# Pairs of tokens side by side in a result, and one store of 128 partitions for each result

## The chip, the cores and the metric

The kernel runs on one core of a Trainium2 chip. The metric is the device time of one execution in microseconds. Before the change the median of three runs is 188.31 us, and the runs lie between 187.92 and 189.54 us. The profile shows one further execution, which took 188.43 us.

## The reference, cut to what matters

```
kv  = einsum('bhsd,bhse->bhde', k, v)          # 8 batches, 8 heads, 576 tokens, 64 per head
o   = einsum('bhsd,bhde->bhse', q, kv)
a   = o / sqrt(mean(o*o, -1) + 1e-6) * g_norm  # per token and head
x   = a with the heads of a token side by side # 4608 tokens x 512
h   = x @ w_in                                 # 512 x 1024
u   = h * softmax(h)
ln  = (u - mean(u)) / sqrt(var(u) + 1e-6) * g_ln
out = ln @ w_out                               # 1024 x 512, float32
```

## The kernel before, in words

The 4608 tokens are worked through in nine chunks of 512. Chunk c from 0 to 7 is a batch without the last ninth of its tokens: the 576 tokens of a batch are read as 64 rows p of nine tokens j, and the chunk holds the tokens with j from 0 to 7. The tokens with j = 8 of all eight batches are copied into q_last and make chunk 8. A chunk has two halves of heads (hf) and two halves of tokens (z or g, the parity of j).

The order of all work is written out by hand, as a list of words called ORDER: each engine's instructions stand in the order of this list, so every queue is in order and a piece that waits holds what is behind it on its engine. A second list, HOME, gives each tile of PSUM one of eight banks. A tile waits for the tile that had its bank before.

A chunk passes these steps, with their words in ORDER and their lines:

- *q*, *k*, *v* (L318) are loads that POOL issues, and they cast to bf16. *kv_mm* (L378) makes kv, and *kv* copies it to kvd.
- *qT* turns q. For chunks 0 to 4 it is a TensorE transpose (L416). For chunks 5 to 8 it is a DMA transpose on SP's queue (L425).
- *o_mm* (L443) makes o, transposed: a head's 64 values in partitions, tokens in columns. For chunks 0 to 7 one product writes 256 columns (four j by 64 p), for chunk 8 it writes 64.
- *sq* squares o on ScalarE (L236), *s_mm* (L501) takes means over a head by a product, *ln* (L505) and *ex* (L509) make the reciprocal root on ScalarE, and *x* (L521) multiplies o, g_norm and this root on VectorE and writes x in bf16.
- *h* is the product with w_in. In chunks 0 to 3 (L574) x is the moving operand and d_ff lies in partitions. In chunks 4 to 8 (L603) x is the stationary operand and tokens lie in partitions.
- *exp* or *expt* (L581, L611) on ScalarE and *u* or *ut* (L585, L617) on VectorE make u. *usq* (L238) and *es* (L598) on POOL, *sums* (L685) on TensorE, or *bn* (L623) on VectorE, make the statistics, *stats* and *rstd* the factor of each token.
- *turnu* (L639) turns u by DMA, in two halves, for chunks 4 to 8, on SP's queue.
- *out* (L751) is the product with w_out, in four blocks m of 128 tokens. *ob* scales it by rstd on VectorE (L244) or ScalarE (L242) into a tile of the four buffers ob.
- *store* writes a block to memory. SP issues nearly all of them (L769); three of chunk 8's five are issued from ScalarE's queue (L765).

A block of 128 tokens of chunks 0 to 7 holds two values of j, 64 tokens each, one below the other: partitions 0 to 63 have j = 2(2(m%2)) + m//2, and partitions 64 to 127 have the j that is 2 larger. So a block leaves as two stores of 64 partitions, with rows of 2 KB:

```
for x in range(2):
    j = 2 * (2 * (m % 2) + x) + m // 2
    on[engine].dma_start(
        out[c * S:c * S + S, :].rearrange("(p j) d -> j p d", j=9)[j], t[64 * x:64 * x + 64, :]
    )
```

SP's queue has the stores and the DMA transposes in one order, as ORDER has them.

Of the kernel before, what the change touches and what calls it, by code (L numbers as in the profile page):

```python
# [99 lines left out]
o.5.0.1:7 s.5.0.0:1 s.5.0.1:0 o.5.1.0:1 o.5.1.1:2 s.5.1.0:3 s.5.1.1:0 o.6.0.0:5 o.6.0.1:0 s.6.0.0:1 s.6.0.1:7  # L100
o.6.1.0:7 o.6.1.1:5 s.6.1.0:1 s.6.1.1:0 o.7.0.0:3 o.7.0.1:2 s.7.0.0:6 s.7.0.1:6 o.7.1.0:7 o.7.1.1:5 s.7.1.0:6
s.7.1.1:2 o.8.0.0:4 o.8.0.1:0 s.8.0.0:6 s.8.0.1:1 o.8.1.0:2 o.8.1.1:6 s.8.1.0:3 s.8.1.1:3 h.4.0.0:3 h.4.0.1:3
h.4.1.0:2 h.4.1.1:7 h.4.2.0:1 h.4.2.1:6 h.4.3.0:5 h.4.3.1:6 h.5.0.0:5 h.5.0.1:7 h.5.1.0:0 h.5.1.1:6 h.5.2.0:4
h.5.2.1:5 h.5.3.0:1 h.5.3.1:0 h.6.0.0:2 h.6.0.1:5 h.6.1.0:7 h.6.1.1:0 h.6.2.0:6 h.6.2.1:1 h.6.3.0:3 h.6.3.1:0
h.7.0.0:3 h.7.0.1:1 h.7.1.0:6 h.7.1.1:7 h.7.2.0:0 h.7.2.1:7 h.7.3.0:2 h.7.3.1:0 h.8.0.0:7 h.8.0.1:3 h.8.1.0:3
h.8.1.1:7 h.8.2.0:6 h.8.2.1:1 h.8.3.0:5 h.8.3.1:7 h.0.0:3 h.0.1:4 h.0.2:2 h.0.3:4 h.0.4:0 h.0.5:6 h.0.6:4 h.0.7:5
# [3 lines left out]
out.2.1:5 out.2.2:0 out.2.3:0 out.3.0:3 out.3.1:4 out.3.2:4 out.3.3:2 out.4.0:7 out.4.1:4 out.4.2:0 out.4.3:3  # L110
out.5.0:5 out.5.1:7 out.5.2:2 out.5.3:3 out.6.0:6 out.6.1:0 out.6.2:5 out.6.3:1 out.7.0:5 out.7.1:0 out.7.2:3
out.7.3:1 out.8.0:5 out.8.1:1 out.8.2:7 out.8.3.0:5 out.8.3.1:7 s.warm:3
# [10 lines left out]
TOKA = ()  # L123

# [53 lines left out]
def kernel(  # L178
# [131 lines left out]
    def heads(c):  # L310
        return (slice(0, 4), slice(4, 8)) if c < 2 else (slice(0, 8),)

    def part_of(c, hf):
        return hf if c < 2 else 0
# [48 lines left out]
    def kv_pairs(b, x):  # L363
        return slice(2 * x, 2 * x + 2) if b < 2 else slice(x, NP, 2)
# [4 lines left out]
    def kv_mm(b, xs):  # L369
        for m in range(2):  # L370
            for i in range(9):
                for x in xs:
                    n = range(NP)[kv_pairs(b, x)][m]
                    for r in range(2):
                        rows = slice(64 * r, 64 * r + 64)
                        for w in range(2) if b < 2 else (0,):
                            y = r ^ (w if b < 2 else x)
# [6 lines left out]
    def kv_copy(engine, b, x, part):  # L384
        if b < 2:
            copy(engine, kvd[:, b, part, kv_pairs(b, x), :], T[kv_key(b, x, part)][:, :, :])
            return
# [7 lines left out]
    def kv_parts(b):  # L395
        return range(2 if b < 2 else 3)

    for b in range(B):
        for xs in ((0,), (1,)) if b < 2 else ((0, 1),):
            g = xs[0]  # L400
            key = {(x, part): kv_key(b, x, part if b < 2 else 0) for x in xs for part in kv_parts(b)}
# [32 lines left out]
    def o_mm(c, hf):  # L434
        qT = T["qT", c]
        for pp in range(2):
            n = 2 * hf + pp
            for y in [slice(0, 4)] if c < B else range(4):
                for hh in range(2):
                    for g in range(2):  # L440
                        first = q_block(c, n, g)
                        rows = slice(64 * g, 64 * g + 64)
                        nc.tensor.matmul(  # L443
                            bank(("o", c, hf, g), [128, 2, 4, 64])[hh * 64:hh * 64 + 64, pp, y, :],
# [23 lines left out]
    def ot_sum(c, y2):  # L468
        sq, s = T["rst", ("sq", c, y2)], kept_tile(("es", ("ss", c, y2)), [128, 2, H, D // 2], FP32)
        a, width = sq, D // 2  # L470
        while width:
            nc.gpsimd.tensor_tensor(out=s[:, :, :, 0:width], in0=a[:, :, :, 0:width], in1=a[:, :, :, width:2 * width], op=ADD)
            a, width = s, width // 2

    def ot_rsqrt(c, y2):
        s, rh = T["es", ("ss", c, y2)], kept_tile(("rh", (c, y2)), [128, 2, H], FP32)
        nc.scalar.activation(out=rh[:, :, :], in_=s[:, :, :, 0], func=AF.Ln, scale=1.0 / D, bias=eps_t[:, :])
# [17 lines left out]
    def o_sq(engine, *i):  # L495
        t = kept_tile(("osq", i), [128, 512], BF16)
        square(engine, t[:, :], T[("o", *i)].rearrange("p a b c -> p (a b c)"))
# [9 lines left out]
    def s_exp(*i):  # L507
        t = kept_tile(("rst", i), [128, 2, 4, 64], FP32)
        nc.scalar.activation(  # L509
            out=t.rearrange("p a b c -> p (a b c)"), in_=T["lss", i][:, :], func=AF.Exp, scale=-0.5, bias=zero_t[:, :]  # L510
        )

    def s_rsqrt(*i):
        t = kept_tile(("rst", i), [128, 2, 4, 64], FP32)
        nc.scalar.activation(
            out=t.rearrange("p a b c -> p (a b c)"), in_=T["s", i][:, :], func=AF.Abs_reciprocal_sqrt, bias=eps_t[:, :]
        )

    def x_mul(c, hf, z):
        t = kept_tile(("x", c), [128, NP, 2, 4, 64], BF16)  # L520
        nc.vector.scalar_tensor_tensor(  # L521
            out=t[:, 2 * hf:2 * hf + 2, z], in0=T["o", c, hf, z][:, :, :, :], scalar=g_rep,
            in1=T["rst", (c, hf, z)][:, :, :, :], op0=MUL, op1=MUL,
# [4 lines left out]
    for c in range(NC):  # L528
# [3 lines left out]
        if c in TOKA:  # L532
            for y2 in range(2):
# [7 lines left out]
                add(("rh", c, y2), "act", lambda _, a=(c, y2): ot_rsqrt(*a), [("ssum", c, y2), "table"], [ss, rh])  # L541
# [6 lines left out]
        for hf in range(2):  # L548
# [5 lines left out]
            kvs = [("kv", b, x, part) for b in ([c] if c < B else range(B)) for x in ((hf,) if b < 2 else range(2))  # L554
# [17 lines left out]
    def h_mm(c, f, dts):  # L572
        for dt in dts:
            nc.tensor.matmul(  # L574
                bank(("h", c, f), [128, 512])[:, :], w_in_sb[:, dt, f * 128:(f + 1) * 128],
                T["x", c][:, dt].rearrange("p a b c -> p (a b c)"), start=(dt == 0), stop=(dt == NP - 1),
# [23 lines left out]
    def ht_mm(c, m, g):  # L600
        x = T["x", c]
        for dt in range(NP):
            nc.tensor.matmul(  # L603
                bank(("h", c, m, g), [128, 512])[:, :], x[:, NP * (m ^ 2 * odd(c, dt)) + dt, :] if c in TOKA else
                x[:, dt, m // 2 ^ odd(c, dt), 2 * (m % 2):2 * (m % 2) + 2, :].rearrange("p b c -> p (b c)"),
# [150 lines left out]

    def scale(engine, key, cols):
        c, m = key[1:3]
        t = kept_tile(("ob", c, m), [128, d_model], FP32)
        times(engine, t[:, cols], T[key][:, cols], T["rstd", c][:, m:m + 1])  # L760

    def store(engine, c, m, cols):
        t = T["ob", c, m]
        if c == LAST:
            on[engine].dma_start(out.rearrange("(r j) d -> j r d", j=9)[8, 128 * m:128 * m + 128, cols], t[:, cols])  # L765
            return
        for x in range(2):
            j = 2 * (2 * (m % 2) + x) + m // 2
            on[engine].dma_start(  # L769
                out[c * S:c * S + S, :].rearrange("(p j) d -> j p d", j=9)[j], t[64 * x:64 * x + 64, :]  # L770
            )
# [77 lines left out]
```

## Time and profile before

| | |
|---|---|
| profiled execution, whole | 188.43 us |
| its span, in which the profile has instructions | 186.7 us |
| TensorE matmul busy | 171.0 us (92%) |
| ScalarE busy | 143.7 us (77%) |
| VectorE busy | 134.9 us (72%) |
| POOL busy | 73.2 us (39%) |
| mean granted TensorE clock | 0.997 |
| stores from SP, count and size | 65 issues (64 of L769), 128 KB at the median |
| stores from SP, issue to landing, median | 2.7 us |
| DMA transposes of u, issue to landing, median | 4.4 us |
| L521, the product that makes x | 36 times, 746 ns in the mean |

The span is counted from the first instruction to the last that the profile shows. The rest of the execution, 1.7 us, lies around it. Busy shares are means over the whole span, and the stages differ; the views by window tell them apart. A row of the timeline gives the start, the duration, the engine, the line, the operation with its operands, the count, and in brackets how long the engine was idle before it and what ended that.

### The profile page before, as it was taken

Reading aid. Unit: us, or ns where it says so; the run is one execution under the profiler, and the core shown is the slowest. Engines: PE = TensorE matmul, PEld = TensorE weight load, DVE = VectorE, ACT = ScalarE, POOL = GpSimd, SP = SyncE. Lnnn points to the kernel's source line nnn. Section 1 sums busy time; section 2 is a strip of 40 time slices with the busy share of each in tenths; the row PEclk is TensorE's granted clock in tenths of the full one; section 3 lists DMA queues with packets and bytes.
Section 4 is the critical chain, followed back from the end, with each engine's and each line's share of the span. In section 5 each row is a group of like instructions: output and inputs, shape, how many; then the busy total and the mean of one; then the engine's idle time right before and its main releaser. Section 6 shows DMA issues by size and latency. Waiting matters only on the chain.

```text
span 186.7 us, 4938 instructions
## 1 busy us (share of the span) xinstructions
PE 171.0 (92%) x1985; PEld 84.6 (45%) x2007; DVE 134.9 (72%) x280; ACT 143.7 (77%) x282; POOL 73.2 (39%) x88
## 2 busy tenths in 40 slices
PE   7968899799999999999967899999999999999890
PEld 5455354255454464444523454444444444444350
DVE  1035567998648976878448968999898899999500
ACT  2437899889788999899968799898989869572351
POOL 7743049998599693998970200000000000000000
PEclk9999999999999999999999999999999999999998
DMA  5999999999999999939969974965979672959994
GB/s 203 284 207 210 207 338 283 210 205 209 208 210 206 274 236 150 205 66 163 222 178 137 285 135 87 202 135 112 210 151 191 122 177 59 211 124 199 188 237 168
DMA packets 50139, 35.48 MB, mean 190 GB/s; under 512 B 31548, under 2 KB 43332, under 8 KB 50116
## 3 DMA queue, kind: packets, MB, share of 16 engines
q0 software_dynamic: 13552, 16.42, 50.2%
q1 hardware_dynamic: 36132, 18.10, 43.0%
q10 hardware_dynamic: 432, 0.66, 1.0%
q8 instruction: 15, 0.25, 0.5%
q14 instruction: 8, 0.07, 0.1%
HBM read 32.51 MB, written 9.44 MB: 225 GB/s over the span
## 4 chain that ended last, share of the span: by engine, by line
PE 55%; DMA 26%; POOL 6%; ACT 4%; DVE 3%; issue 3%; SPq 1%; ACTq 0%; POOLq 0%
PE out_ps L751 25%; PE h_ps L603 13%; DMA w_in_sb<-in_moe_w_in_dram 8%; PE h_ps L574 7%; DMA q_sb<-in_q_dram 5%; DMA v_sb<-in_v_dram 5%; DMA qT_sb<-q_sb 4%; DMA w_sb<-u_sb 3%; PE s_ps L501 3%; PE misc_ps L685 2%; ACT e_sb L581 2%; PE o_ps L443 2%; PE misc_ps L378 2%; PE misc_ps L416 2%; DMA out_dram<-ob_sb 1%
## 5 line engine op out<-in xcount | busy, mean ns | idle before, releaser
L603 PE MATMUL h_ps<-w_in_sb,x_sb 128*128 128x512 bf16 x153 | 37.8, 379 | 0.5 <-issue 0.2
L751 PE MATMUL out_ps<-w_out_sb,w_sb 128*128 128x512 bf16 (+1 forms) x166 | 37.3, 369 | 0.6 <-DMA w_sb<-u_sb 0.4
L611 ACT ACTIVATE e_sb<-h_ps,zero_t 128x512 f32<-128x512 f32 x40 | 27.2, 682 | 8.2 <-PE h_ps L603 7.6
L521 DVE SCALAR_TENSOR_TENSOR x_sb<-o_ps,g_cols,rst_sb 128x512 bf16<-128x512 f32 x36 | 26.5, 746 | 9.2 <-ACT rst_sb L509 7.6
L751 PE MATMUL out_ps<-w_out_sb,u_sb 128*128 128x512 bf16 x122 | 30.8, 379 | 2.0 <-ACT lss_sb L505 1.7
L574 PE MATMUL h_ps<-x_sb,w_in_sb 128*128 128x512 bf16 x122 | 31.2, 380 | 1.4 <-DMA w_in_sb<-in_moe_w_in_dram 0.5
L238 POOL TENSOR_TENSOR usq_sb<-u_sb 128x512 bf16<-128x512 bf16 x27 | 27.4, 1040 | 9.7 <-DVE u_sb L585 9.7
L617 DVE TENSOR_TENSOR u_sb<-h_ps,e_sb 128x512 bf16<-128x512 f32 x40 | 26.8, 683 | 2.0 <-ACT e_sb L611 1.8
L623 DVE BATCH_NORM_STATS2 bn_sb<-u_sb 128x6 f32<-128x512 bf16 x40 | 26.6, 685 | 0.4
L236 ACT ACTIVATE osq_sb<-o_ps,zero_t 128x512 bf16<-128x512 f32 x36 | 23.2, 688 | 4.3 <-PE o_ps L443 4.1
L585 DVE TENSOR_TENSOR u_sb<-h_ps,e_sb 128x512 bf16<-128x512 f32 x32 | 21.4, 687 | 6.5 <-ACT e_sb L581 6.2
L505 ACT ACTIVATE lss_sb<-s_ps,eps_t 128x512 f32<-128x512 f32 x32 | 21.9, 688 | 4.0 <-PE s_ps L501 3.7
L751 PEld LDWEIGHTS <-w_sb 128*128 128x128 bf16 x168 | 16.1, 98 | 19.1 <-DMA w_sb<-u_sb 1.5
L603 PEld LDWEIGHTS <-x_sb 128*128 128x128 bf16 x160 | 15.3, 98 | 18.7 <-issue 0.4
L509 ACT ACTIVATE rst_sb<-lss_sb,zero_t 128x512 f32<-128x512 f32 x32 | 23.0, 722 | 0.6
L581 ACT ACTIVATE e_sb<-h_ps,zero_t 128x512 f32<-128x512 f32 x32 | 21.3, 689 | 2.7 <-PE h_ps L574 2.5
L598 POOL TENSOR_TENSOR es_sb<-e_sb 128x512 bf16<-128x512 f32 x16 | 20.2, 1276 | 5.5 <-ACT e_sb L581 5.3
L242 ACT ACTIVATE ob_sb<-out_ps,rstd_sb 128x512 f32<-128x512 f32 (+1 forms) x18 | 11.6, 661 | 10.3 <-PE out_ps L751 5.8
L751 PEld LDWEIGHTS <-u_sb 128*128 128x128 bf16 x128 | 12.1, 98 | 15.8 <-issue 2.5
L574 PEld LDWEIGHTS <-w_in_sb 128*128 128x128 bf16 x128 | 11.3, 97 | 15.7 <-issue 2.7
L244 DVE TENSOR_SCALAR ob_sb<-out_ps,rstd_sb 128x512 f32<-128x512 f32 x19 | 14.0, 744 | 5.2 <-ACT rstd_sb L708 2.0
L501 PE MATMUL s_ps<-osq_sb,head_mean 128*128 128x512 bf16 x35 | 13.1, 380 | 0.5 <-DVE u_sb L585 0.3
(72 smaller groups left out, 159.6 us busy)
## 6 DMA issues: line engine op xcount, KB each, us to landing
out_dram<-ob_sb SPq DMA_DIRECT2D x65, 128.0 KB, 2.7
k_sb<-in_k_dram POOLq DMA_DIRECT2D x6, 576.0 KB, 10.2
v_sb<-in_v_dram POOLq DMA_DIRECT2D x6, 576.0 KB, 10.6
q_sb<-in_q_dram POOLq DMA_DIRECT2D x6, 576.0 KB, 10.7
w_sb<-in_moe_w_out_dram POOLq DMA_DIRECT2D x2, 1024.0 KB, 15.5
w_in_sb<-in_moe_w_in_dram POOLq DMA_DIRECT2D x2, 512.0 KB, 13.9
v_sb<-in_v_dram POOLq DMA_DIRECT2D x3, 288.0 KB, 11.2
q_sb<-in_q_dram POOLq DMA_DIRECT2D x3, 288.0 KB, 10.5
```

The lines of the kernel that those rows point to most:

```text
L236: nc.scalar.activation(out=dst, in_=src, func=AF.Square, bias=zero_t[:, :])
L238: on[engine].tensor_tensor(out=dst, in0=src, in1=src, op=MUL)
L505: nc.scalar.activation(out=t[:, :], in_=T["s", i][:, :], func=AF.Ln, bias=eps_t[:, :])
L509: nc.scalar.activation(out=t.rearrange("p a b c -> p (a b c)"), in_=T["lss", i][:, :], func=AF.Exp, scale=-0.5, bias=zero_t[:, :])
L521: nc.vector.scalar_tensor_tensor(out=t[:, 2 * hf:2 * hf + 2, z], in0=T["o", c, hf, z][:, :, :, :], scalar=g_rep, in1=T["rst", (c, hf, z)][ ...
L574: nc.tensor.matmul(bank(("h", c, f), [128, 512])[:, :], w_in_sb[:, dt, f * 128:(f + 1) * 128], T["x", c][:, dt].rearrange("p a b c -> p (a ...
L581: nc.scalar.activation(out=t[:, f % 2, :], in_=T["h", c, f][:, :], func=AF.Exp, bias=zero_t[:, :])
L603: nc.tensor.matmul(bank(("h", c, m, g), [128, 512])[:, :], x[:, NP * (m ^ 2 * odd(c, dt)) + dt, :] if c in TOKA else x[:, dt, m // 2 ^ odd ...
L611: nc.scalar.activation(out=t[:, g, :], in_=T["h", c, m, g][:, :], func=AF.Exp, bias=zero_t[:, :], accum_out=se[:, m, g:g + 1])
L617: nc.vector.tensor_tensor(out=t[:, m, g * 512:(g + 1) * 512], in0=T["h", c, m, g][:, :], in1=T["e", c, m][:, g, :], op=MUL)
L623: nc.vector.bn_stats(out=t[:, m, g, :], in_=T["u", c][:, m, g * 512:(g + 1) * 512])
L751: nc.tensor.matmul(bank(key, [128, d_model])[:, cols], T["w", c][:, m, f, :] if c in TOKS else T["u", c][:, f, m * 128:(m + 1) * 128], w_o ...
```

## The change

Tokens of a block are ordered in pairs: partition 2p + w holds row p and the w-th of the block's two values of j. The product that makes x does this ordering. The o tile is laid out by w first, o_mm writes its 256 columns as runs of 64 into this layout, and the product reads it straight and writes bf16 at a step of two elements, for w = 0 and then w = 1. The tile x is laid out by token half first, so h reads two runs of 256 as its moving operand, or 128 columns on end as its stationary one.

A block is then 64 rows of two tokens each, and one store of 128 partitions takes it. The scaled results of chunks 3 to 8 go to the buffers of k and v, four each, by the parity of m; those of chunks 0 to 2 stay in the four of ob. Chunk 8's tokens are paired in the same way, by batch. HOME is changed for part of the tiles from chunk 5's and 4's on; seven tiles get another tile ahead of them in their bank (h.4.0.1, h.4.1.0, h.4.2.1, h.4.3.0, out.3.1, out.8.3.0 and out.8.3.1). ORDER stays as it is, and each engine has its instructions in the same order as before, with 32 stores fewer on SP's queue. The rest of the difference is in branches that this kernel does not take (TOKA is empty), and HALVES has a name where c < 2 stood.

```diff
@@ o_mm
-                        nc.tensor.matmul(
-                            bank(("o", c, hf, g), [128, 2, 4, 64])[hh * 64:hh * 64 + 64, pp, y, :],
+                        t = bank(("o", c, hf, g), [128, 2, 2, 2, 64])[hh * 64:hh * 64 + 64, :, pp]
+                        nc.tensor.matmul(
+                            t.rearrange("e w v p -> e v w p") if c < B else t[:, y % 2, y // 2],
@@ x_mul
-        t = kept_tile(("x", c), [128, NP, 2, 4, 64], BF16)
+        t = kept_tile(("x", c), [128, 2, NP, 256], BF16)
         nc.vector.scalar_tensor_tensor(
-            out=t[:, 2 * hf:2 * hf + 2, z], in0=T["o", c, hf, z][:, :, :, :], scalar=g_rep,
-            in1=T["rst", (c, hf, z)][:, :, :, :], op0=MUL, op1=MUL,
+            out=t[:, z, 2 * hf:2 * hf + 2].rearrange("p a (vt w) -> p w (a vt)", w=2),
+            in0=T["o", c, hf, z].rearrange("p w a v t -> p w (a v t)"), scalar=g_rep,
+            in1=T["rst", (c, hf, z)].rearrange("p (w t) -> p w t", w=2), op0=MUL, op1=MUL,
         )
@@ h_mm
-                T["x", c][:, dt].rearrange("p a b c -> p (a b c)"), start=(dt == 0), stop=(dt == NP - 1),
+                T["x", c][:, :, dt, :], start=(dt == 0), stop=(dt == NP - 1),
@@ ht_mm
-                x[:, dt, m // 2 ^ odd(c, dt), 2 * (m % 2):2 * (m % 2) + 2, :].rearrange("p b c -> p (b c)"),
+                x[:, m // 2 ^ odd(c, dt), dt, 128 * (m % 2):128 * (m % 2) + 128],
@@ scale and store
+    def ob_key(c, m):
+        return ("ob", c, m) if c < 3 else ("kv"[m % 2], ("ob", c, m))
+
     def scale(engine, key, cols):
         c, m = key[1:3]
-        t = kept_tile(("ob", c, m), [128, d_model], FP32)
+        t = kept_tile(ob_key(c, m), [128, d_model], FP32)
         times(engine, t[:, cols], T[key][:, cols], T["rstd", c][:, m:m + 1])
 
     def store(engine, c, m, cols):
-        t = T["ob", c, m]
+        t = T[ob_key(c, m)]
+        first = 4 * (m % 2) + m // 2
+        rows = out[c * S:c * S + S, :].rearrange("(p j) d -> p j d", j=9) if c < B else None
         if c == LAST:
-            on[engine].dma_start(out.rearrange("(r j) d -> j r d", j=9)[8, 128 * m:128 * m + 128, cols], t[:, cols])
-            return
-        for x in range(2):
-            j = 2 * (2 * (m % 2) + x) + m // 2
-            on[engine].dma_start(
-                out[c * S:c * S + S, :].rearrange("(p j) d -> j p d", j=9)[j], t[64 * x:64 * x + 64, :]
-            )
+            last = out.rearrange("(b p j) d -> p b j d", p=64, j=9)[:, 2 * m:2 * m + 2, 8, cols]
+            ...
+                on[engine].dma_start(last, t[:, cols])
+        elif c not in TOKA:
+            on[engine].dma_start(rows[:, first:first + 3:2, :], t[:, :])
...
```

## The prediction

> **What bounds the kernel now.** I read the page first, then the table of windows, the chain that ended last, the idle gaps in TensorE's timeline, and then each queue at those gaps. The busy shares alone say TensorE; the windows say where it is not TensorE.
>
> ```profile
> PE 171.0 (92%) x1985; PEld 84.6 (45%) x2007; DVE 134.9 (72%) x280; ACT 143.7 (77%) x282; POOL 73.2 (39%) x88
> ...
> 38.00:85.97 47.97, 47.05 (x792) 24.14 (x789) 37.29 (x76) 43.01 (x81) 39.74 (x42) 1.00 1.10 197
> 85.97:103.00 17.03, 13.95 (x150) 6.43 (x148) 11.40 (x23) 14.36 (x27) 10.05 (x11) 1.00 0.94 170
> 103.00:176.40 73.40, 72.72 (x487) 33.05 (x496) 67.17 (x139) 56.16 (x128) 1.08 (x3) 1.00 0.79 161
> 114.00:172.00 58.00, 57.63 (x335) 25.82 (x339) 55.14 (x111) 46.18 (x107) 0.00 (x0) 1.00 0.75 150
> ```
>
> The columns of the last four lines are window, length, then busy time of PE, PEld, DVE, ACT and POOL, granted clock, DMA share, GB/s. From 38 to 86 us and from 103 to 176 us TensorE is busy 98 to 99% of the time at full clock, so nothing that speeds up a queue can gain there. Between 86 and 103 us it loses 3.1 us. VectorE is busy 55.1 of 58.0 us from 114 to 172 us: it has 2.9 us to spare, no more.
>
> The gaps in TensorE's timeline after 38 us, and the chain through them:
>
> ```profile
> 96.12 1.89 PE L751 MATMUL out_ps<-w_out_sb,u_sb 128*128 128x512 bf16 x8 [1.67 <-ACT lss_sb L505]
> 103.01 0.41 PE L443 MATMUL o_ps<-qT_sb,kvd 64*64 64x256 bf16 x8 [1.34 <-DMA qT_sb<-q_sb]
> 176.79 5.37 PE L751 MATMUL out_ps<-w_out_sb,w_sb 128*128 128x512 bf16 x32 [0.42 <-DMA w_sb<-u_sb]
> ```
>
> ```profile
> 83.53 2.44 POOL es_sb L598 x2
> 85.97 8.94 DMA q_sb<-in_q_dram
> 94.96 8.01 DMA qT_sb<-q_sb
> 103.01 0.41 PE o_ps L443 x8
> ```
>
> The first gap (1.67) is ScalarE's lateness, and ScalarE had waited for a store to land (next fence). But curing it alone gains nothing: TensorE then reaches o_mm.6.0 earlier and waits there, because the chain at that place is the load of q.6, its transpose qT.6, and only then TensorE. The second gap (1.34) shows that TensorE is the one that waits. The third gap is 0.42 us before the last result.
>
> Who made ScalarE late, and what a store costs SP's queue:
>
> ```profile
> 94.80 0.69 ACT L242 ACTIVATE ob_sb<-out_ps,rstd_sb 128x512 f32<-128x512 f32 x1 [1.78 <-DMA out_dram<-ob_sb]
> ```
>
> ```profile
> 85.62 5.33 SPq L769 DMA_DIRECT2D out_dram<-ob_sb  x8
> 94.96 2.70 SPq L425 DMA_TRANSPOSE qT_sb<-q_sb  x1
> ```
>
> ```profile
> L769 SPq DMA_DIRECT2D out_dram<-ob_sb x64: 466/588/836, 56.9 to 179.6; - x64
> ```
>
> **The change, part by part.** Stores: 64 issues of L769 at a median 588 ns become 32. That takes 32 x 0.588 = 18.8 us out of SP's queue, where the transposes stand too. Only what lies in front of a late transpose, or frees a buffer that is waited for, can reach the end.
>
> (a) *86 to 103 us.* In this stretch eight store issues (1 MB) share the 16 DMA engines with the load of q.6. How much engine time a store takes, I read from two stretches:
>
> ```profile
> 146.50:156.00 9.50, 9.45 (x45) 4.28 (x45) 8.57 (x20) 7.76 (x19) 0.00 (x0) 1.00 0.63 140
> 180.00:185.00 5.00, 2.16 (x18) 1.57 (x16) 0.00 (x0) 1.67 (x4) 0.00 (x0) 1.00 0.82 270
> ```
>
> In the first, only stores of 64 partitions run: 9.50 x 0.63 = 6.0 us of all engines for 10 of them, 1.20 us per result of 256 KB. In the second, mostly stores of 128 partitions: 5.00 x 0.82 = 4.1 us for 1.35 MB, 0.80 us per 256 KB. So four results save about 1.6 us of engine time; load and stores interleave and end together near 94.9 us, so I give the load half, 0.8 us. Then qT.6 issues at 94.2 instead of 94.96. Its transfer takes 8.01 us where an undisturbed one took 4.7 (the least of this line), since the load of q.7, issued on POOL at 95.84 and unmoved, joins after some 1.6 us (the load of q.6, issued at 85.97, showed in the traffic at 87.6). So 2.5 of its 4.7 us were done undisturbed, and the other 2.2 took 5.5 us: a rate of 0.4. Starting 0.8 us earlier, 3.3 are done and 1.4 remain, 3.5 us: it lands at 100.95 instead of 102.97, 2.0 us earlier. TensorE must be there: it now starts to wait at 101.67, and is there at 100.9 if 0.8 of ScalarE's 1.67 us goes. Of a result's two issues one goes, so the store that ScalarE waited for is issued 1.2 us earlier; that suffices. Taken: 2.0 us. Bounds: 0 (the load lands no earlier), 3.0 (both gaps), and a loss where stores queued sooner hold the load back (a rival below).
>
> By the Trainium skill, "SBUF — State Buffer", section Door 1: The DMA port swizzle, a transfer of 64 partitions reaches half the ports that one of 128 does (196 against 328 GB/s at 1 MiB). By that rule 1.20 us would become 0.72, and this term would be some 2.3 us; the rows' 0.80 is used.
>
> (b) *176.4 us.* The transpose of u.8's first half waits on SP behind the second issue of store.6.0: its input is written at 170.78, it issues at 172.03. One issue less puts it 0.6 us earlier, more than the gap of 0.42 us. Gain 0.4 (0 to 0.42).
>
> (c) *The tail.* TensorE ends at 182.16, ScalarE's last scale at 182.99, because four scales wait 2.5 us in all for buffers whose stores are behind eight issues (5.21 us from 175.13). Results of chunks 3 to 8 now use the eight freed buffers of k and v, so no scale waits; the last 0.42 us scale starts as TensorE ends. Gain 0.35 (0 to 0.4). What follows (issue 0.34, landing 2.3, end) stays.
>
> (d) *The product that makes x*, 36 times, writes bf16 at a step of two elements. No row has that. The nearest is L244: 744 ns for 512 results that advance 4 bytes each, as these now do, against 746 ns for L521 itself. I take 0. Upper bound: a second pass over 512 elements at the slope between the casts of 128 columns (286 ns) and the products of 512 (683): 1.03 ns x 512 = 0.53 us. Lower bound 0: it reads as much as before.
>
> (e) *TensorE's o products* write 256 columns as four runs of 64, and h reads x as two runs of 256. The sums of L685 read runs of 32 and run 80 in 1.23 us, so short runs in a read cost nothing. For the write, o_mm of chunk 8 writes runs of 64 in 32 small products, 0.38 us a half against 0.34 for eight large ones; so between 0 and 0.04 us a half, 14 of them after 38 us: 0 to 0.6, taken 0.
>
> (f) *New homes of PSUM tiles* change whom seven tiles wait for. Five are near 93 to 104 us, ahead of the wait for qT.6 that covers them; the latest owner, x.5.0.0, ends at 99.60 and its heir starts at 99.78. Two are the last halves of chunk 8, where out.8.3.1 now waits for ob.8.0, done at about 179.5, before TensorE is there at 179.9. Uncovered, each would cost a few tenths. Taken 0.
>
> Sum, against the profiled execution's 188.43 us (span 186.70 and 1.73 around it, 0.1 above the median of 188.31): 188.43 - 2.0 - 0.4 - 0.35 = **185.7 us**, 1.4% below the median.
>
> **Rivals.** *The load keeps its time* (0.28). It lands 8.94 us after issue, and an undisturbed load of this size needed long as well: the row gives a median of 10.7 us. If HBM reads set it, qT.6 lands at 103.0 as before; the ScalarE wait that goes turns into a longer wait there. Against it: loads and stores visibly share engines at 0.94. Time: 188.43 - 0.75 = 187.7, within 1%.
>
> *The stores hold the load back* (0.17), the slower side. With one issue per result, all four of a chunk stand in the rings by 88 us, not 90.9, just as the load begins. If the fuller ring wins, the load lands later. At 1.2 us later qT.6 starts at 96.2, has 1.3 us done before q.7's load joins, and needs 3.4/0.4 = 8.5 more: 105.9, 3.0 us late. 188.43 + 3.0 - 0.75 = 190.7. From 0.3 us later on, it eats (b) and (c). Against it: the bytes are the same.
>
> *The strided write costs* (0.07). Ten products lie from 114 to 172 us; at 0.53 us they add 5.3 to a VectorE with 2.9 to spare: +2.4, decisive from 0.29 us each. With (a) failing it is 190.1, with (a) 188.1.
>
> *Runs in PSUM cost* (0.03). Were each o group twice as long, 12 groups of chunks 2 to 7 add 4.1 us to a full TensorE: 189.8. The Trainium skill, "PSUM — Partial Sum Buffer", section Specifications (TRN2), says any non-contiguous pattern slows matmuls significantly; the 0.38 us of chunk 8 speaks against so much here.
>
> **How the numbers follow.** The forecast has 0.45. A measurement of this kernel tells about 1% from no change, 1.9 us either way. Faster by more: the forecast, 0.45. Within: 0.28 from the load that keeps its time. Slower: 0.17, 0.07, 0.03, their sum 0.27. Range: low is all three gains at their bounds, 188.43 - 3.0 - 0.42 - 0.4 = 184.6; high takes in most of the slower cases, 190.4. The forecast's own range is 184.6 to 186.5.
>
> **What would show it.** Right: 32 stores on L769's successor near 0.59 us each; qT.6 landing near 101; no wait of a scale for a store after 110 us; L521's successor at 740 to 750 ns. Wrong: the load of q.6 still taking 8.9 us or more, a wait of TensorE for qT.6 of 3 us, or the product above 1 us.

## The result and the profile after

The changed kernel takes 191.68 us in the median of 20 executions (189.19 to 194.53), the kernel before beside it 188.36 us in the median of 20 (186.57 to 192.09). The ratio is 1.0142, with a 95% interval from 1.0108 to 1.0176: slower by 1.4%. (The ratios here leave out executions more than 1.5% above the fastest of their kernel, so they can differ a little from those of the medians.) The profiled execution of the changed kernel took 189.19 us, one of its two fastest, with a span of 187.3 us. So the question has two parts: why this execution is not faster than the 188.43 us of the profile before, and why most others are 2 us slower still.

Line numbers have moved: L521 is L529 now, L574 L584, L603 L613, L751 L761, L769 L786, L425 L426, L443 L445. The page and the table of windows, whose columns are as before:

```profile
PE 171.0 (91%) x1989; PEld 84.7 (45%) x2007; DVE 135.8 (73%) x280; ACT 143.7 (77%) x282; POOL 73.2 (39%) x88
...
L529 DVE SCALAR_TENSOR_TENSOR x_sb<-o_ps,g_cols,rst_sb 128x512 bf16<-128x512 f32 x36 | 28.1, 788 | 9.4 <-ACT rst_sb L517 7.1
```

```profile
38.00:88.34 50.34, 48.00 (x844) 24.69 (x851) 38.34 (x77) 43.71 (x83) 40.42 (x43) 1.00 1.08 195
88.34:104.78 16.44, 13.76 (x151) 6.46 (x150) 12.72 (x25) 14.49 (x28) 10.05 (x11) 1.00 0.85 164
104.78:177.98 73.20, 72.62 (x488) 33.23 (x498) 66.16 (x138) 55.84 (x127) 1.08 (x3) 1.00 0.70 165
115.50:173.50 58.00, 57.68 (x336) 26.02 (x341) 55.21 (x111) 46.32 (x107) 0.00 (x0) 1.00 0.63 153
148.00:157.50 9.50, 9.45 (x45) 4.32 (x45) 8.59 (x20) 7.76 (x19) 0.00 (x0) 1.00 0.36 140
```

The first three end at the same pieces of work as before, the last two are those of before moved by 1.5 us. The first took 47.97 us and takes 50.34; TensorE is idle in it for 2.3 us where it was for 0.9. The other 0.9 us of it is work that was done before 38 us there: the product of k and v at L379, behind the load of v, starts at 38.34, in the profile before at 37.41. The second is 0.6 us shorter. The third is as long as before. The last line holds five results with one store each: 9.50 x 0.36 = 3.4 us of all DMA engines, 0.68 us a result, against 1.20 before. The product that makes x takes 788 ns, against 746.

TensorE's gaps, the chain through the one at qT.6, and SP's queue there. In the second fence, "issue" is time in which the engine waited for nothing that the profile shows:

```profile
22.73 2.75 PE L584 MATMUL h_ps<-x_sb,w_in_sb 128*128 128x512 bf16 x12 [0.95 <-DVE x_sb L529]
...
58.16 0.59 PE L584 MATMUL h_ps<-x_sb,w_in_sb 128*128 128x512 bf16 x2 [0.93 <-DVE x_sb L529]
...
104.78 0.41 PE L445 MATMUL o_ps<-qT_sb,kvd 64*64 64x256 bf16 x8 [2.60 <-DMA qT_sb<-q_sb]
...
169.98 13.35 PE L761 MATMUL out_ps<-w_out_sb,w_sb 128*128 128x512 bf16 x67
```

```profile
96.78 0.35 PE out_ps L761 x2
97.14 7.60 DMA qT_sb<-q_sb
104.73 0.04 issue
104.78 0.41 PE o_ps L445 x8
```

```profile
87.24 2.52 SPq L786 DMA_DIRECT2D out_dram<-ob_sb  x4
97.14 2.71 SPq L426 DMA_TRANSPOSE qT_sb<-q_sb  x1
```

The two gaps of 1.67 and 1.34 us have become one of 2.60 us: ScalarE no longer waits for a store, so TensorE is early at o_mm.6.0 and waits there. The gap of 0.42 us before the last result is gone: the last row shows 67 products on end. Two gaps of 0.9 us before L584 are there that end on the product that makes x; at the place of the first, profiles of other kernels show a wait of 0.4 to 1.3 us for the load of w_in.

Against the profile before, o_mm.6.0 starts 1.77 us later, L761's run for the last chunk 1.55 us later (169.98 against 168.43), TensorE ends 1.17 us later and the span 0.6 us later. So 0.22, 0.38 and 0.53 us are won behind o_mm.6.0, and 1.77 us are lost ahead of it. Not all of the 1.77 need be the change: o_mm.2.0, at 42.98 in the profile before and at 44.14 here, is at 43.73 in a second profile of the kernel before.

### The profile page after: what moved, and what is told of

Read it like the earlier page. It is cut to its first block, busy times and chain, and to the rows that moved or that the text cites. A ratio compares the mean times of both kernels' runs of the same rounds, so it can differ in the third digit from the quotient of the medians.

```text
span 187.3 us, 4900 instructions
## 1 busy us (share of the span) xinstructions
PE 171.0 (91%) x1989; PEld 84.7 (45%) x2007; DVE 135.8 (73%) x280; ACT 143.7 (77%) x282; POOL 73.2 (39%) x88
## 4 chain that ended last, share of the span: by engine, by line
PE 67%; DMA 16%; ACT 5%; POOL 5%; DVE 4%; issue 2%; POOLq 0%; DVEq 0%; ACTq 0%
PE out_ps L761 29%; PE h_ps L613 17%; PE h_ps L584 9%; DMA v_sb<-in_v_dram 6%; DMA q_sb<-in_q_dram 5%; DMA qT_sb<-q_sb 4%; PE s_ps L509 3%; PE misc_ps L695 3%; PE o_ps L445 3%; PE misc_ps L379 2%; DVE x_sb L529 2%; ACT lss_sb L513 1%; ACT e_sb L591 1%; PE misc_ps L417 1%; ACT rst_sb L517 1%
## 5 line engine op out<-in xcount | busy, mean ns | idle before, releaser
L613 PE MATMUL h_ps<-w_in_sb,x_sb 128*128 128x512 bf16 x153 | 37.8, 379 | 0.5 <-issue 0.2
L761 PE MATMUL out_ps<-w_out_sb,w_sb 128*128 128x512 bf16 (+1 forms) x166 | 37.3, 369 | 0.1
L529 DVE SCALAR_TENSOR_TENSOR x_sb<-o_ps,g_cols,rst_sb 128x512 bf16<-128x512 f32 x36 | 28.1, 788 | 9.4 <-ACT rst_sb L517 7.1
L584 PE MATMUL h_ps<-x_sb,w_in_sb 128*128 128x512 bf16 x128 | 32.0, 380 | 2.6 <-DVE x_sb L529 2.4
L761 PE MATMUL out_ps<-w_out_sb,u_sb 128*128 128x512 bf16 x120 | 30.8, 379 | 0.4
L761 PEld LDWEIGHTS <-w_sb 128*128 128x128 bf16 x168 | 16.2, 98 | 18.4 <-issue 0.4
L613 PEld LDWEIGHTS <-x_sb 128*128 128x128 bf16 x160 | 15.3, 98 | 18.7 <-issue 0.4
L584 PEld LDWEIGHTS <-w_in_sb 128*128 128x128 bf16 x128 | 11.5, 97 | 17.5 <-issue 4.5
L761 PEld LDWEIGHTS <-u_sb 128*128 128x128 bf16 x128 | 12.1, 98 | 14.0 <-issue 0.6
L233 DVE CAST kvd<-misc_ps 64x128 bf16<-64x128 f32 (+1 forms) x27 | 7.5, 287 | 5.8 <-PE misc_ps L379 4.7
L445 PE MATMUL o_ps<-qT_sb,kvd 64*64 64x256 bf16 (+1 forms) x192 | 7.3, 251 | 3.4 <-DMA qT_sb<-q_sb 2.6
```

The costliest lines, as they stand in the source:

```text
L529: nc.vector.scalar_tensor_tensor(out=t[:, z, 2 * hf:2 * hf + 2].rearrange("p a (vt w) -> p w (a vt)", w=2), in0=T["o", c, hf, z].rearrange ...
L584: nc.tensor.matmul(bank(("h", c, f), [128, 512])[:, :], w_in_sb[:, dt, f * 128:(f + 1) * 128], T["x", c][:, :, dt, :], start=(dt == 0), st ...
L613: nc.tensor.matmul(bank(("h", c, m, g), [128, 512])[:, :], x[:, NP * (m ^ 2 * odd(c, dt)) + dt, :] if c in TOKA else x[:, m // 2 ^ odd(c, ...
L761: nc.tensor.matmul(bank(key, [128, d_model])[:, cols], T["w", c][:, m, f, :] if c in TOKS else T["u", c][:, f, m * 128:(m + 1) * 128], w_o ...
```

## The experiments

All comparisons are with the kernel before, run beside the others on the same chip. There were five such batches on five chips; the changed kernel was not run again in them, so its comparison with an edited kernel goes through the kernel before. I also give how many executions had a mean granted TensorE clock of 0.994 or more, called "clock kept" below, since this splits them: of the kernel before 101 of 138 did (15 of 24 to 18 of 21 by batch), with a median span of 186.0 us, and 37 did not, with 189.9 us. Of the changed kernel only 2 of 20 did (187.3 us; the other 18: 189.4 us), and none of those 18 was profiled. The line is a little too strict: the mean takes in the time after TensorE's last product too, and a mean of 0.993 can come from there alone (in one profile below the clock is full up to 183.2 us, and the last product ends at 181.1).

**The kernel before again** (no edit).

> The kernel before, unchanged, to have the granted clock and span of each of its runs: the changed kernel's runs lie at granted clocks of 0.978 to 1.0 and 189.2 to 194.5 us, its profiled one at 1.0 and 189.19. If the clock is lowered by the change (theory: throttle), these runs of before keep 0.995 or more in nearly all runs and lie near 188.4 us. If the clock varies by itself and falls on both kernels alike (rival), they too lie between 0.98 and 1.0, with spans that go with it, and the ratio to before is 1.00 within 0.3%.

Measured: 188.95 us, ratio 1.0004 (0.9948 to 1.0059), clock kept in 8 of 12. So the clock varies in the kernel before too, but it is kept far oftener than in the changed kernel. Its profiled execution had a clock of 0.987, and shows what such an execution is. TensorE's timeline, and windows of one microsecond (columns: window, length, PE busy, granted clock, DMA share, GB/s):

```profile
97.73 3.13 PE L751 MATMUL out_ps<-w_out_sb,u_sb 128*128 128x512 bf16 x8 [2.19 <-ACT lss_sb L505]
```

```profile
96.00:97.00 1.00, 0.00 (x0) 1.00 0.06 23
97.00:98.00 1.00, 0.27 (x2) 1.00 0.63 125
98.00:99.00 1.00, 1.00 (x5) 0.61 1.12 213
99.00:100.00 1.00, 1.00 (x4) 0.50 1.01 186
100.00:101.00 1.00, 1.00 (x3) 0.50 1.28 98
101.00:102.00 1.00, 1.00 (x5) 0.69 0.82 112
102.00:103.00 1.00, 1.00 (x6) 1.00 1.25 160
```

ScalarE's wait for a store was longer here, and TensorE's gap 2.19 us instead of 1.67. Right behind it the granted clock is at half for 3.4 us: 0.39 + 0.50 + 0.50 + 0.31 = 1.7 us of work are lost. This became the clock theory: a gap of some 2 us costs the clock as well, and the change makes such a gap in most executions.

**x as two tiles** by half of the heads, and the same with a plain (dense) write, which leaves the pairing of the tokens out:

```diff
-        t = kept_tile(("x", c), [128, 2, NP, 256], BF16)
+        t = x_half(c, hf)        # one [128, 2, 2, 256] tile for each half of the heads
...
-            out=t[:, z, 2 * hf:2 * hf + 2].rearrange("p a (vt w) -> p w (a vt)", w=2),
+            out=t[:, z].rearrange("p a (vt w) -> p w (a vt)", w=2),   # dense: out=t[:, z],
```

> The changed kernel with x in two tiles, one for each half of the heads, so that a product of one half and the h products that read the other half share no tile. Theory false wait: the interleaved layout makes x.0.1.0 wait for h.0.x.0 and h.2.1.0 wait for x.2.1.0 although they touch different columns; the gaps of 0.6 us in VectorE before x.0.1.0 and of 0.93 us in TensorE before h.2.1.0 go, o_mm.6.0 starts near 103.2 instead of 104.8, and the time falls by 1.2 to 1.8 us against the changed kernel, to 1.004 to 1.008 of before. Rival strided write: only the 42 ns a product matter, gaps shrink by no more than 0.3 us, and the time stays at 1.012 to 1.016 of before.

> As the one before, and the product that makes x writes its 512 bf16 results one after the other instead of at a step of two. The order of the tokens in x is then mixed up, so this leaves out the pairing; all sizes and counts stay. The product should go back from 788 to about 746 ns. Theory false wait: the time is within 0.3 us of the kernel with x in two tiles. Rival strided write: it is 1 us or more faster than that one, and at or under the kernel before.

Measured: 190.02 us, ratio 0.998 (0.9908 to 1.0052), and 189.74 us, ratio 1.0032 (0.998 to 1.0085). The product takes 789 ns in the first and 746 in the second, so the step of two elements costs 43 ns; the kernels' times do not show it. Both ratios are lower than the changed kernel's 1.0142, the medians are not lower than that of the kernel before (188.83 us beside them). What the split takes away is a wait. In the changed program, h.2.1.0 reads heads of half 0 alone, yet waits for x.2.1.0, the product of half 1, which stands right ahead of it in ORDER; likewise x.0.1.0 and x.1.1.0 wait for products of h that read the other half. The strided write into the common tile counts as touching columns that it does not write. With two tiles, or with a dense write into one, these waits are not in the program. The traces agree: from o_mm.2.1 to o_mm.3.1, with x.2.1.0 and h.2.1.0 in between, it takes 7.65 to 8.09 us in the five profiled kernels with one tile and the strided write, and 6.21 to 7.06 us in all others, those before the change among them. TensorE's timeline of the split kernel:

```profile
56.50 0.59 PE L589 MATMUL h_ps<-x_sb,w_in_sb 128*128 128x512 bf16 x2
57.03 0.41 PE L445 MATMUL o_ps<-qT_sb,kvd 64*64 64x256 bf16 x8
...
103.43 0.43 PE L445 MATMUL o_ps<-qT_sb,kvd 64*64 64x256 bf16 x8 [2.42 <-DMA qT_sb<-q_sb]
104.20 3.98 PE L617 MATMUL h_ps<-w_in_sb,x_sb 128*128 128x512 bf16 x11 [0.34 <-issue]
```

h.2.1.0 is 1.66 us earlier than in the changed kernel, 0.61 us of which it had at o_mm.2.1 already, with no gap ahead of it. But the gap before o_mm.6.0 is still there, and the eleven products behind it take 3.98 us instead of 2.54. Their windows (columns as above):

```profile
103.00:104.00 1.00, 0.43 (x8) 0.85 1.14 274
104.00:105.00 1.00, 0.80 (x2) 0.50 1.14 247
105.00:106.00 1.00, 1.00 (x4) 0.50 1.10 292
106.00:107.00 1.00, 1.00 (x4) 0.50 1.08 404
107.00:108.00 1.00, 1.00 (x5) 0.94 0.37 133
```

Only 3 of 12 and 5 of 12 executions kept a clock of 0.994. In those the median spans are 185.4 and 185.7 us, about that of the kernel before.

**Two stores for a result** in the changed kernel:

```diff
-            on[engine].dma_start(rows[:, first:first + 3:2, :], t[:, :])
+            for x in range(2):
+                on[engine].dma_start(rows[32 * x:32 * x + 32, first:first + 3:2, :], t[64 * x:64 * x + 64, :])
```

> The changed kernel with each result of chunks 0 to 7 stored by two stores of 64 partitions again (32 rows of two tokens each); all else as changed. It tells what the halving of the stores is worth. By the prediction's terms, two stores cost 0.4 us at the last transpose and 0.3 us or less in the tail, and up to 2 us at the load of q.6: 1.5 to 2.7 us more than the changed kernel. Rival: the stores are off the path, since the load of q.6 took 8.8 us with half the stores as it took 8.9 with all: 0 to 0.5 us more than the changed kernel.

Measured: 188.92 us, ratio 1.0036 (0.999 to 1.0081), and the clock was kept in 11 of 12. ScalarE's wait for a store is back, 0.93 us, and splits the gap: 0.90 us there, none to speak of at o_mm.6.0:

```profile
97.38 1.89 PE L761 MATMUL out_ps<-w_out_sb,u_sb 128*128 128x512 bf16 x8 [0.90 <-ACT lss_sb L513]
...
103.15 0.41 PE L445 MATMUL o_ps<-qT_sb,kvd 64*64 64x256 bf16 x8
```

Putting the stores back costs nothing and gives back most of the loss. That fits the clock theory, but a wait and the stores changed together. (Its kept executions have a median span of 186.6 us, the changed kernel's two 187.3.)

**Products of zeros in the gap.** The edit, eight or four of them:

```diff
-FILL = {... 7: ("h.0.2", 4, 512)}
+FILL = {... 7: ("h.0.2", 4, 512), 8: ("o.6.0.0", 8, 512)}
-... expt.4.2.1 o_mm.6.0 ut.4.2.1
+... expt.4.2.1 warm.8 o_mm.6.0 ut.4.2.1
```

> The changed kernel with eight products of a block of zeros (128x512, 0.216 us each, 1.73 us together) put into TensorE's order right before o_mm.6.0, so that its wait for qT.6 is no longer one empty stretch of 2.4 to 3.7 us. Theory (clock): the merged wait is what lowers the granted clock a few microseconds later, in most runs of the changed kernel; with the products in it the mean granted clock stays at 0.994 or more in nearly all runs (it was so in 2 of 20 of the changed kernel), and the median time falls by some 2 us to 189.2, the time that the changed kernel's own full-clock runs give; still about 0.5% above the kernel before. Rival (the VectorE work alone): the low clock is chance, the products change neither it nor the time: 191.5. Second rival: the products delay o_mm.6.0 and what follows: over 192.

> The changed kernel with four products of zeros (0.86 us) before o_mm.6.0 in place of eight: they leave 1.6 us or more of the stretch empty. If the length of the empty stretch decides, with a limit between 1.7 us (held in the kernel before) and 2.4 us (fell in the split kernel), the clock is at 0.994 or more in most runs (8 of 12 or more) and the time is 189.0 to 189.8. If any empty stretch there lowers the clock, or the products only helped by their number: clock below 0.993 in most runs and 191.

Measured: with eight 189.26 us, ratio 1.0066 (1.0021 to 1.0111), clock kept in 11 of 12; with four 189.99 us, ratio 1.0031 (0.9986 to 1.0076), clock kept in 7 of 12. So the clock was kept in 2 of 20, 7 of 12 and 11 of 12 for none, four and eight. With useless work on the waiting engine the changed kernel's median is 2.4 us lower; by the ratios, 1.0142 and 1.0066, it is 1.4 us, and their intervals just touch. That fits the clock theory. The limit of 8 with four products was missed by one. The profiled execution with four ran at a granted clock of 0.851 from 4 us on and took 205.26 us; why is not known, and its trace is left out below where I say so.

**Two tiles and the products of zeros:**

> The changed kernel with x as two tiles by head half (no wait of one half's product for reads of the other half) and the eight products of zeros before o_mm.6.0. If both the waits of the single tile and the clock are the loss: clock 0.994 or more in nearly all runs, and the time is that of the split kernel's full-clock spans (184.6 to 185.7) with 1.7 around them: 187.2, ratio to the kernel before 0.994. If the clock falls for another reason: as the split kernel without the products, 190.0.

Measured: 189.73 us, ratio 0.9997 (0.9942 to 1.0051), clock kept in 9 of 12. The clock is back in most, the forecast time of 187.2 is not.

**The wait taken from the kernel before**, by other means, without and with the products:

```diff
+    def ob_key(c, m):
+        return ("ob", c, m) if c != 2 else ("kv"[m % 2], ("ob", c, m))
...
-        t = kept_tile(("ob", c, m), [128, d_model], FP32)
+        t = kept_tile(ob_key(c, m), [128, d_model], FP32)
```

> The kernel before with one thing changed: the four result buffers of chunk 2 lie in slots of k and v, so that no ScalarE scale waits for a store around 93 to 95 us. Two stores of 64 partitions for each result and the plain product as before. Clock theory: ScalarE's 1.8 us wait goes, TensorE's two empty stretches of 1.67 and 1.34 us become one of 2.5 or more before o_mm.6.0, the clock falls under 0.993 in most runs and the time rises by 1 to 2 us, to 189.5 to 190.5, though a wait was taken away and nothing added. Rival (a wait less is a gain, or is worth nothing): 187 to 188.4, and the clock as in the kernel before (0.994 or more in two thirds of the runs).

> The run before it, with the eight products of zeros before o_mm.6.0 as well. Clock theory: the merged stretch is filled, the clock is at 0.994 or more in nearly all runs, and the time is that of the kernel before at full clock or a little under, 187.2 to 187.9. Rival: as without the products, whatever that is.

> The kernel before with chunk 2's result buffers in slots of k and v once more, for the trace of an execution at full clock: the one profiled so far had a clock of 0.976, an empty TensorE stretch of 3.94 us before o_mm.6.0 and a clock of 0.50 from the stretch's third microsecond on, but 10 of 13 executions stayed at 0.994 or more. If the length of the stretch decides (clock theory), a profiled execution at full clock shows a stretch before o_mm.6.0 of less than 2.4 us, because qT.6 lands earlier against TensorE's work than in the changed kernel. If it shows 2.6 us or more at full clock, length alone does not decide.

Measured: 187.26 us without the products, ratio 0.9958 (0.9922 to 0.9994), and 187.78 with them, ratio 1.0003 (0.9968 to 1.0038). The clock was kept in 10 of 13 and 9 of 12 (two more of the 12 had 0.993, and the profiled one of these two is full up to 183.2 us). The repeat without them had 185.37 and 192.14 us. This is a miss for the theory as I had put it: in the kernel before, taking the wait away was no loss. The two executions that were profiled (spans of 190.7 and 190.4 us) do show the long gap and the clock behind it; the first:

```profile
104.42 0.64 PE L443 MATMUL o_ps<-qT_sb,kvd 64*64 64x256 bf16 x8 [3.94 <-DMA qT_sb<-q_sb]
```

```profile
102.00:103.00 1.00, 0.00 (x0) 0.97 1.18 159
103.00:104.00 1.00, 0.00 (x0) 0.50 1.18 202
104.00:105.00 1.00, 0.58 (x8) 0.50 1.13 310
```

The gap begins at 100.48 and the clock falls at about 102.9, 2.5 us into it, while TensorE still waits. An execution of this kernel at full clock was not profiled, so how long its gap is stays open; spans down to 183.6 us, 2.4 under the median of the kernel before at full clock, suggest that qT.6 lands early in them.

**A plain write in one tile, with the products; and the form of the store once more:**

> The changed kernel with a plain (dense) write of the product that makes x, so the tokens of a result are not paired; the eight products of zeros before o_mm.6.0 are in. One store for each result stays. It leaves the strided write and the waits that came with it out, and the clock's fall too. Theory: what the changed kernel loses beside the clock is the write and its waits: full-clock time 187.0 to 187.7, ratio to the kernel before 0.995 to 1.0, and h.2.1.0 no longer 2.6 us late. Rival (the stores of 128 partitions themselves cost time): 188.5 to 189.2, as the changed kernel with the same products (189.26).

> As the run beside it (plain write of the product, so tokens are not paired; eight products of zeros before o_mm.6.0), with each result's rows in two stores of 64 partitions on SyncE instead of one of 128. Nothing else differs. Theory (stores): one store of 128 partitions puts the four results of chunk 1 behind each other within 2.5 us right at the issue of q.6's load (two stores spread them over 5.3 us), the load or qT.6's transfer lands later in most executions, and that is the 1 us left at full clock; with two stores the time falls by about 1.5 us to 188.0 and o_mm.6.0 starts 14 us after o_mm.4.0's line (13.6 to 14.1 in profiles of filled kernels with two stores) rather than 16.2. Rival (the form of the store does not matter; the landing varies by itself): the two runs agree within 0.5 us.

> The plain write with the eight products of zeros and one store of 128 partitions for each result once more, on the chip and beside the runs of its two-store form. Both theories: 189.0 to 189.9 as before.

> The changed kernel with x in two tiles, the eight products, and two stores of 64 partitions for each result. Theory (stores): 1 to 1.5 us under its one-store form run beside it, 187.5 to 188.3. Rival: within 0.5 us of it.

> The changed kernel with x in two tiles and the eight products, one store for each result, beside its two-store form. Both theories: 188.7 to 189.7 (it had 189.73, and 188.71 at full clock).

Measured: 189.63 us for the plain write (ratio 1.0078, 1.0034 to 1.0122), where I had given 187.0 to 187.7; clock kept in 9 of 12, and the profiled execution has a gap of 2.15 us behind the zeros and the clock at half after it. (Where the expectation says o_mm.4.0, the piece is o_mm.5.0.) Then, six executions each, 191.02 with two stores against 189.98 with one (ratios 1.0166, 1.0111 to 1.022, and 1.0108, 1.0055 to 1.016; clock kept in 5 and 2 of 6), and in the split kernel, ten and twelve executions, 189.42 against 189.52 (1.0083, 1.0042 to 1.0124, and 1.0063, 1.0016 to 1.0111; clock kept in 9 of 10 and 9 of 12). Two stores are not faster in either pair: the theory that the stores hold the load back falls. What these kernels have in common is the products, and they do not keep the clock in every execution. In the split kernel with two stores:

```profile
101.39 1.89 PE L829 MATMUL o_ps<-zeros 128*128 128x512 bf16 x8
103.21 0.41 PE L445 MATMUL o_ps<-qT_sb,kvd 64*64 64x256 bf16 x8
```

Its qT.6 was issued at 94.63 and landed 6.9 us later, at 101.5; o_mm.6.0 had to wait for the zeros until 103.21. So where qT.6 lands early the products cost up to 1.7 us, all eight of them.

**Real products in the gap.** Eight products that followed o_mm.6.0 go ahead of it:

```diff
-... expt.4.2.1 o_mm.6.0 ut.4.2.1 expt.4.2.0 bn.4.2.1 sq.6.0.1 h.4.0.1 expt.4.0.1 sq.6.0.0 ... bn.4.3.0 h.4.1.1
+... expt.4.2.1 ut.4.2.1 expt.4.2.0 bn.4.2.1 h.4.0.1 expt.4.0.1 h.4.1.1 o_mm.6.0 sq.6.0.1 sq.6.0.0 ... bn.4.3.0
```

> The changed kernel with x in two tiles, and no products of zeros: eight real products that stood right behind o_mm.6.0 in TensorE's order (h.4.0.1 and h.4.1.1, 1.73 us) stand ahead of it. They fill the empty stretch with work that is due anyway, so nothing is added. Theory: the clock is at 0.994 or more in 9 of 12 runs or more (as with the products of zeros), and the price of those products, up to 1.7 us where qT.6 lands early, is saved: span 184.5 to 185.7, time 186.7 to 187.4, 0.994 of the kernel before. Rival (something of the change costs 1 us beside the waits and the clock): 188.5 to 189.5 as with the products of zeros.

> The kernel before with chunk 2's result buffers in slots of k and v (no scale waits for a store) and the same move of eight products ahead of o_mm.6.0. Theory: clock 0.994 or more in nearly all runs, 186.5 to 187.2; it shows what the cured ScalarE wait is worth in the kernel before once the empty stretch is gone. Rival: 187.8, as with the products of zeros.

> The changed kernel as it is, with the move of eight products ahead of o_mm.6.0 alone. Theory: the clock comes back as with the products of zeros (11 of 12 runs), and the time is that of the split kernel with the move plus the 1.0 to 1.3 us of the single tile's waits: 187.8 to 188.7. Rival: 189.3, as with the products of zeros.

Measured:

| | median us (n) | ratio to before | clock kept | span where kept |
|---|---|---|---|---|
| split, with the move | 186.43 (6) | 0.9893 (0.9825 to 0.9961) | 3 of 6 | 183.5 |
| before, buffers of chunk 2 moved, with the move | 186.72 (12) | 0.9928 (0.9887 to 0.997) | 9 of 12 | 184.6 |
| changed, with the move | 188.97 (12) | 0.998 (0.9925 to 1.0036) | 6 of 12 | 184.6 |

The first and the second beat both kernels. The stretch in the split kernel with the move:

```profile
98.81 3.62 PE L617 MATMUL h_ps<-w_in_sb,x_sb 128*128 128x512 bf16 x15
102.74 0.41 PE L445 MATMUL o_ps<-qT_sb,kvd 64*64 64x256 bf16 x8 [0.32 <-DMA qT_sb<-q_sb]
```

The rival, that something else in the change costs 1 us, falls. That it was the zeros fits, but is not shown to the microsecond: where the clock is kept, the split kernel's median span was 186.6 and 187.0 us with them and is 183.5 with the move (three executions), on three chips, and the zeros are 1.7 us of work. Between the first and the third row lies the single tile with its waits: 1.1 us of span where the clock is kept, 2.5 us in the medians. The move alone mended the changed kernel's clock in half its executions, not in 11 of 12 as I expected; its executions with a lower clock were not profiled, so where it fell in them is not known. That it need not be at o_mm.6.0 shows the profiled execution of the second row (clock 0.991): there the clock is at half from 40.89 to 44.30 us, behind a gap of 2.60 us in which TensorE waited for the load of v until 39.88, and full from there to 187 us. And the move itself is worth something in any kernel, 1.7 us of work done in the gap, so the first row is not the worth of the pairing: between the first row and the second, which has no pairing, no difference can be told. No run had the move alone in the kernel before.

## Why the prediction was wrong, step by step

The forecast was 185.7 us, 2.75 under the profiled execution before; that of the changed kernel is 0.76 above it, and the median another 2.5 above that.

(a) *86 to 103 us: wrong, the largest term.* Its premise held and more: a store's engine time fell from 1.20 to 0.68 us a result. The failed step is "I give the load half". From the issue of q.6's load to that of qT.6 it took 8.94 us in the mean of ten profiled executions of kernels with one store (8.42 to 9.65; without the one at a clock of 0.851, which had 6.39), and 8.66 in nine with two (7.55 to 9.76). The load does not land earlier, and so neither does qT.6: from the issue of q.6 to qT.6's landing it took 16.55 and 16.46 us in the mean. In the one pair of profiles, 17.00 became 16.39, 0.2 us of it from the load and 0.4 from qT.6's transfer, well within the spread. Of the gain of 2.0, nothing is left in the means. Why the load gets none of the engine time that came free is open. By the Trainium skill, "SBUF — State Buffer", section Door 1: The DMA port swizzle, 128 partitions reach twice the ports of 64; the 0.68 agrees with that, and it was still worth nothing on this path.

(b) *0.42 us before the last result: right.* The gap is gone; 0.38 us were won there.

(c) *The tail: right.* No scale waits for a store; from TensorE's end to the end of the span it is 3.96 us against 4.49, 0.53 won where 0.35 was forecast.

(d) *The product at a step of two: near.* 42 ns, not 0, and far from the bound of 0.53 us. From 115.5 to 173.5 us TensorE is busy 57.68 of 58.0 us, so VectorE's 2.9 us in hand covered it there.

*Missing altogether: the waits that the new write brings.* I costed the product's duration and not whom it waits for. One tile for both halves of the heads plus a strided write made TensorE and VectorE wait for each other between 22 and 58 us. By o_mm.5.0, at 87 to 90 us, four profiled kernels with the single tile and the strided write stand at 89.5 in the mean (89.16 to 89.85; without the one at a clock of 0.851), five with the split tile and the strided write at 88.1 (87.67 to 88.69). That is 1.4 us, most of it between o_mm.2.1 and o_mm.3.1, and it was in the program before it ran.

(e), (f) *Runs in PSUM and new homes:* nothing in the traces speaks against 0 for these; no run tried them alone.

*The rivals.* "The load keeps its time" came true as a mechanism, with the very words "the ScalarE wait that goes turns into a longer wait there". Its price was wrong, since I priced the longer wait at nothing. A wait of 1.67 and one of 1.34 us, with work between them, left the clock alone; of ten unbroken waits of 2.15 us or more, nine did not. In the changed kernel itself no fall of the clock was profiled; it is argued from its executions' means and from filling the gap, after which 191.68 became 189.26 us. "The stores hold the load back" gave 190.7, nearest to the outcome, and was tried and fell: no run shows a part of the stores in it.

What stays open: why the kernel before without its ScalarE wait keeps its clock so much oftener than the changed kernel (10 of 13 against 2 of 20), when its gap in a full-clock execution was never seen, nor that of the changed kernel in one with a lower clock. How the clock falls is less open than it looked; the last section has it.

## What to carry to other kernels

Before a wait on one engine is cured, ask which wait takes its place and how long the waiting TensorE will then stand empty in one piece: two short gaps can be cheaper than one long one, and work that is due anyway, put ahead of the waiting piece, is the cure for both. When a write changes its pattern or its tile, list whom its readers and writers wait for in the built program before and after; a strided write into a shared tile can tie halves together that were free. A resource that is relieved, here 0.5 us of DMA time a result, is worth something only if the transfer that is waited for is seen to move with it.

## What the runs showed of the hardware

The granted clock fell to 0.50 behind every unbroken TensorE gap of 2.15 us or more that the traces have between 20 us and the last product, but one: 2.15 us (plain write with eight products), 2.19 (the kernel before again), 2.40 (plain write with eight products, two stores), 2.42 (split), 2.58 (split with eight products), 2.60 (the kernel before with the move), 2.94 and 3.94 (the kernel before without the ScalarE wait) and 3.74 (split, plain write). The one is the gap of 2.60 us in the profiled execution of the changed kernel. It stayed up after 1.67 and 1.34 us in the kernel before.

What tells them apart is a grid in time. Up to TensorE's last product, each stretch of half clock lasts 3.41 us or twice that, and in each trace it begins a whole number of 3.41 us after the first record of the clock (in the split kernel 99.0 us, 29 of them). Cut each trace into these windows, without the one at a clock of 0.851, and the time in which TensorE is empty within one window decides. Examples:

| kernel | window, us | TensorE empty in it, us | clock in the next |
|---|---|---|---|
| before | 93.46 to 96.88 | 1.67 | 1.00 |
| changed | 99.76 to 103.17 | 0.99 | 1.00 |
| changed | 103.17 to 106.59 | 1.77 | 1.00 |
| plain write, eight products | 101.57 to 104.98 | 2.15 | 0.50 |
| split, eight products | 101.20 to 104.61 | 2.58 | 0.50 |

In 19 traces, the clock fell after all 22 full-clock windows with 2.12 us or more empty, those after the last product counted too, and after none of the 971 with 1.99 us or less. The changed kernel's gap of 2.60 us was cut in two by the edge at 103.17 us, so that it cost no clock. The grid's first edge lies anywhere from 3.96 to 6.75 us in the traces, so a gap of between 2 and 4 us can cost the clock in one execution and not in the next. That fits kernels that show both, and it is why many executions are needed to compare two of them.

The Trainium skill, "TensorE: Matmul & The Clock Gate", section Part 1: The HAM clock gate, tells of a window of about 3.4 us that runs freely, with half the clock after one idle window; its table of rules asks for no idle gap of more than about 3 us. The traces agree in the half clock and in the window that runs freely; they differ in size, since a window with 2.12 us empty was enough, and so were gaps of 2.15 us.

A bf16 write at a step of two elements from VectorE's product of 512 columns took 788 ns against 746, so the step is not free, but nearly so. The load of q.6 and qT.6's transfer together took between 14.0 and 21.1 us in 19 profiled executions, in kernels that issue them alike; this spread is larger than most of the effects that were looked for here.
